# Four maxima in a row, numerators bank by bank, and the first loads on one queue, in an attention and MoE kernel

## The chip, the cores and the metric

The kernel runs on one core of a Trainium2 chip. The metric is the device time of one execution in microseconds. The core has a matrix engine (TensorE, PE in the profile; its weight loads are the row PEld), a vector engine (VectorE, DVE), a scalar engine (ScalarE, ACT), a general one (GpSimd, POOL) and a sequencer that issues transfers (SyncE, SP). Each engine runs its own list of instructions in order, and waits for semaphores of the others. Matmul results lie in PSUM, in banks of 128 x 512 f32 numbers; DVE and ACT read them there.

## The reference

Random-feature attention over 8 batches, 8 heads and 576 tokens, and behind it a mixture of experts in which each token takes one expert:

```python
q_s, k_s = (q * scale, k * scale)
def phi(x):
    h = np.einsum('bhsd,md->bhsm', x, omega) - np.sum(x * x, axis=-1, keepdims=True) / 2.0
    return np.exp(h - np.max(h, axis=-1, keepdims=True)) / np.sqrt(m)
q_p, k_p = (phi(q_s), phi(k_s))
kv = np.einsum('bhsm,bhsd->bhmd', k_p, v)
z = np.sum(k_p, axis=2)
num = np.einsum('bhsm,bhmd->bhsd', q_p, kv)
den = np.einsum('bhsm,bhm->bhs', q_p, z)[..., None] + 1e-06
x = (num / den), heads side by side: 4608 tokens x 512
# MoE: expert_idx = argmax(xn @ en.T / tau); out = gate * (relu(x @ w1[e]) @ w2[e])
```

Per head, omega is 128 x 64: the projection of a token has 128 features. The sum of squares drops out, since the maximum is taken away.

## The kernel before, in words

The 4608 tokens are 36 tiles of 128. Phase 1 is a loop of steps (L623 to L702). Step `i` works on the keys of tile `i` and on the queries of tile `iq = i - 6` (`LAG` is 6), and finishes the numerators of tile `iq - 2`. The eight heads of a tile are two groups of four, `a` = 0 and 1, and each group fills one PSUM bank: 4 x 128 features. So a full step has four banks of projections, here called k0, q1, k1 and q0 (letter and group). The order on each engine is the order of the code, with nothing that reorders it in the loop (`manual_schedule`).

In one full step the engines do this:

- PE: projections of k0 and q1, then of k1 and q0 (`proj`, L322); the products k-features x v of the tile before (`kvmm`, L346); now and then small products (`spare`: the routing counts L456 and L458, the transposed kv L366, its logits L377); transposes of the query features (`qtr`, L392), group 0 into the bank `nu[1]`, group 1 into a bank of the tag "py"; the numerators (`num`, L411), group 0 into `nu[0]`, group 1 into `nu[1]`.
- DVE: `num_out` of the tile before (L424 to L431), the maxima of k0 and q1 (L328), then the list `mid` (reads of the small products: L370, L383, L461, or the reduction over logits L442 to L445), then the maximum of k1, the copy of the transposed queries of group 0 (`qcopy`, L400), the maximum of q0, and the list `ends` (L450 to L452, L464 to L474, L357).
- ACT: four exponentials each (`feats`, L331) for k0 and q1, the `qcopy` of group 1 (L398), then the exponentials of k1 and of q0. An exponential needs the maximum of its bank as its bias.

A bank holds what was put there until its reader is done: the numerators of group 1 need the copy L400, since the transposes of group 0 stand in the same bank `nu[1]`; the next projections need the exponentials of the banks whose places they take. When all keys of half a superblock are in, the accumulated kv is copied to `kvs` (L353, on ACT), and its logits follow over three steps (L357, L366, L370, L377, L383).

`num_out` adds a small constant to the denominators of group 0 and of group 1 (L424, twice), takes one reciprocal over both (L425, 128 x 8), and then multiplies, for each group, the logits (L427) and the 256 numerators (L431).

In the first steps there are no queries yet. Before the loop, SP issues the loads of k (L297), one after the other; ACT issues those of omega (`om`, L572, two halves) and of the first four tiles of v (L306). `om` is scaled on DVE (L575) ahead of the first projection. The MoE follows in phase 2, from about 300 us on.

Of the kernel before, what the change touches and what calls it, by code (L numbers as in the profile page):

```python
# [11 lines left out]
F32 = mybir.dt.float32  # L12
# [4 lines left out]
AF = mybir.ActivationFunctionType  # L17
ALU = mybir.AluOpType
# [4 lines left out]
P = 128  # L23
# [30 lines left out]
def attention_moe(ctx: ExitStack, tc: tile.TileContext, qT, kT, v1, omT, emb, tau, w1q, w2q, xs, out):  # L54
# [225 lines left out]
    with ExitStack() as c1:  # L280
# [11 lines left out]
        def load(i):  # L292

            if i >= NTILE:
                return
            st["k", i] = p1.tile([P, 4, P], F32, name=f"kt{i}", tag="qt" if i in (2, 3) else "kt", bufs=2)
            nc.sync.dma_start(st["k", i], kT[i])  # L297
            sb, u = divmod(i, TPS)
            j = sb * (TPS + 1) + u
            for key, r in [("v", j if u < 4 else j + 1)] + [("v0", j)] * (u == 4):  # L300
                if i in (1, 2):
                    vt = rawp.tile([P, F], F32, name=f"vt{i}", tag="raw_w1")[:, 0 : H * (D + 1)].rearrange("p (h d) -> p h d", h=H)
                else:
                    vt = p1.tile([P, H, D + 1], F32, name=f"vt{i}{key}", tag="vt", bufs=3)

                (nc.scalar if i < 4 else nc.sync).dma_start(vt, v1[r])  # L306
                st[key, i] = vt

        def loadq(i):
# [6 lines left out]
        def proj(*which):  # L316
            for w, i, a, tag in which:
                st["pj" + w, i, a] = ps.tile([P, 4, M], F32, name=f"pj{w}{i}_{a}", tag=tag, bufs=2)
            for c in range(4):
                for w, i, a, _ in which:  # L320
                    r = slice(a * D, (a + 1) * D)
                    nc.tensor.matmul(st["pj" + w, i, a][:, c, :], st[w, i][r, c, :], om[r, :], start=True, stop=True)  # L322

        def feats(which, i, a):

            pj = st["pj" + which, i, a]
            nm = small.tile([P, 4], F32, name=f"nm{which}{i}_{a}", tag=f"nm{which}", bufs=4)
            nc.vector.tensor_reduce(nm, pj, axis=AX.X, op=ALU.max, negate=True)  # L328
            ft = p1.tile([P, 4, M], F32, name=f"ft{which}{i}_{a}", tag=f"ft{which}", bufs=3)
            for h in range(4):  # L330
                nc.scalar.activation(ft[:, h, :], pj[:, h, :], AF.Exp, bias=nm[:, h : h + 1])  # L331
            st["f" + which, i, a] = ft

        def kvmm(i, a, b):
            sb, u = divmod(i, TPS)
            ft = st["fk", i, a]
            vt = st["v0", i] if (u, b) == (4, 0) else st["v", i]
            begin = u == 4 * b
            if begin:
                kva[sb, b, a] = ps.tile([P, 4, D + 1], F32, name=f"kva{sb}_{b}_{a}", tag=f"kv{a}")  # L340
            acc = kva[sb, b, a]
            for h in range(4):


                for c in range(0, P, 64):
                    nc.tensor.matmul(  # L346
                        acc[c : c + 64, h, :], ft[:, h, c : c + 64], vt[:, 2 * h + a, :],
                        start=begin and h == 0, stop=u == 4 + 4 * b and h == 3,
                    )
            if u == 4 + 4 * b:  # L350
                if a == 0:
                    kvs[sb, b] = p1.tile([P, H, D + 1 + E], F32, name=f"kvs{sb}_{b}", tag="kvs", bufs=2)
                nc.scalar.activation(kvs[sb, b][:, 4 * a : 4 * a + 4, 0 : D + 1], acc, AF.Copy)  # L353

        def kv_dense(sb, b):
            kvc = rawp.tile([P, F], F32, name=f"kvc{sb}_{b}", tag="raw_w1")[:, 0:DM].rearrange("p (h d) -> p h d", h=H)
# [59 lines left out]
        def num_out(i):  # L416
            g, gi = divmod(i, G)
            st["xr", i] = xr = p1.tile([P, PAY], F32, name=f"xr{i}", tag="xr", bufs=6)
            nc.gpsimd.tensor_copy(xr[:, PAY - 1 :].bitcast(I32), ids[:, i : i + 1])
            if gi == 0:  # L420
                st["lg", g] = small.tile([P, G, H, E], F32, name=f"lg{g}", tag="lg", bufs=1)
            rr = small.tile([P, 2, 4], F32, name=f"rr{i}", tag="rr", bufs=3)
            for a in range(2):
                nc.vector.tensor_scalar(rr[:, a], pn[a][:, :, D], EPS, None, op0=ALU.add)  # L424
            nc.vector.reciprocal(rr, rr)  # L425
            for a in range(2):
                nc.vector.tensor_tensor(  # L427
                    st["lg", g][:, gi, 4 * a : 4 * a + 4],
                    pn[a][:, :, D + 1 :], rr[:, a].unsqueeze(2).to_broadcast([P, 4, E]), op=ALU.mult,
                )  # L430
                nc.vector.tensor_tensor(  # L431
                    xr[:, 0:DM].rearrange("p (h a d) -> p a h d", a=2, d=D)[:, a],
                    pn[a][:, :, 0:D], rr[:, a].unsqueeze(2).to_broadcast([P, 4, D]), op=ALU.mult,
                )
# [133 lines left out]
        c1.enter_context(tc.manual_schedule(engines={ET.PE, ET.Pool}))  # L568

        om = once.tile([P, M], F32, name="om")  # L570
        for a in range(2):
            nc.scalar.dma_start(om[a * D : (a + 1) * D, :], omT)  # L572
        for i in range(4):
            load(i)
        nc.vector.tensor_scalar(om, om, SCALE, None, op0=ALU.mult)  # L575
# [47 lines left out]
        for i in range(NTILE + LAG + 1):  # L623
            iq = i - LAG
            if i < 2 or i >= 4:
                load(i + (4 if i < 2 else 2))
            loadq(iq + 2)
            if iq - 3 * GPICK - 6 == 3:
                prow = [nc.values_load(
                    firsti[0:1, t : t + 1], engines=[ET.SP], min_val=t * P, max_val=(E - 1) * REG + t * P,  # L630
                    skip_runtime_bounds_check_because=WHY) for t in range(NPRE + 1)]
                for t in range(NPRE):
                    xload(t, prow[t], xgp[t])
            ks, qs = i < NTILE, 0 <= iq < NTILE
            if ks and qs:
                pairs = [("k", i, 0, "py"), ("q", iq, 1, "py")], [("k", i, 1, "px"), ("q", iq, 0, "px")]
            elif ks:
                pairs = [("k", i, a, ("px", "py")[i % 2]) for a in range(2)], []
            else:
                pairs = [("q", iq, a, "px") for a in (1, 0)] if qs else [], []  # L640
            filling = i > NTILE
            proj(*pairs[0])
            proj(*pairs[1])
            if later is not None:
                num_out(later)
            for p in pairs[0][: 1 if i < LAG else 2]:
                feats(*p[:3])
            if 0 <= i - 1 < NTILE:
                sb, u = divmod(i - 1, TPS)
                for b in range(2 if i < LAG and u == 4 else 1):  # L650
                    for a in range(2):
                        kvmm(i - 1, a, b or int(u > 4))
            if i < LAG:
                feats(*pairs[0][1][:3])
            late = bool(spare.get((i,)))
            go(spare, i)
            if later is not None and later % G == G - 1 and later < NTILE - 1:
                steps = routed(later // G)

                for d, key in ((mid, i), (ends, i), (spare, i + 1), (mid, i + 1), (ends, i + 1), (ends, i + 2), (ends, i + 3)):  # L660
                    key = min(key, NTILE + LAG)
                    at(d, key).append((next, steps, None))
            go(mid, i)
            if not qs and iq >= 2:
                num(iq - 2)
            if iq >= 1:

                for a in (1, 0) if late else (0, 1):
                    qtr(iq - 1, a, not ks)
                qcopy(iq - 1, 1, True)  # L670
            if 0 <= i - 1 < NTILE and u == 4 and i >= LAG:
                for a in range(2):
                    kvmm(i - 1, a, 1)
            for p in pairs[1][:1]:
                feats(*p[:3])
            if iq >= 1:
                qcopy(iq - 1, 0, False)
            for p in pairs[1][1:]:
                feats(*p[:3])
            if filling:  # L680
                filled(1 if i <= NTILE + 2 else 2)
            if filling:
                filled(1 if i > NTILE + 2 else 0)
            if 0 <= i - 1 < NTILE:
                if u in (4, 8):
                    b = u // 4 - 1
                    at(ends, i).append((kv_dense, sb, b))
                    at(spare, i + 1).append((kv_turn, sb, b))
                    at(mid, i + 1).append((kv_turned, sb, b))
                    at(spare, i + 2).append((kv_logits, sb, b))  # L690
                    at(mid, i + 2).append((kv_logits_out, sb, b))
            later = iq - 2 if iq >= 2 else None
            if qs and iq >= 2:
                num(iq - 2)
            go(ends, i)
            if filling:
                filled(1)
            n = iq - 3 * GPICK - 6
            if 1 <= n < 2 * NQ + 1:
                at(ends, i + 1).append((first_split, n - 1))  # L700
            if 0 <= n < 2 * NQ:
                first_weights(n)  # L702
# [433 lines left out]
```

## Time and profile before

| | us |
|---|---|
| median of 3 runs (714.92 to 718.11) | 716.06 |
| the profiled execution's own time | 715.37 |
| its span in the profile | 713.7 |
| PE busy in the span | 666.7 (93%) |
| DVE busy | 571.1 (80%) |
| ACT busy | 418.2 (59%) |

The span is the time from the first to the last instruction; 1.67 us of the execution lie around it. Busy shares are averages over stages with different limits: the page's 40 slices show PE at nine tenths or more in most of the span, at six and eight in the first two slices, and at seven and eight in five of the slices around the passage from phase 1 to phase 2. Times below are microseconds from the start of the span.

### The profile page before, as it was taken

Reading aid. Unit: us, or ns where it says so; the run is one execution under the profiler, and the core shown is the slowest. Engines: PE = TensorE matmul, PEld = TensorE weight load, DVE = VectorE, ACT = ScalarE, POOL = GpSimd, SP = SyncE. Lnnn points to the kernel's source line nnn. Section 1 sums busy time; section 2 is a strip of 40 time slices with the busy share of each in tenths; the row PEclk is TensorE's granted clock in tenths of the full one; section 3 lists DMA queues with packets and bytes.
Section 4 is the critical chain, followed back from the end, with each engine's and each line's share of the span. In section 5 each row is a group of like instructions: output and inputs, shape, how many; then the busy total and the mean of one; then the engine's idle time right before and its main releaser. Section 6 shows DMA issues by size and latency. Waiting matters only on the chain. (4 is left out here: it accounts for less than half of the span.)

```text
span 713.7 us, 17997 instructions
## 1 busy us (share of the span) xinstructions
PE 666.7 (93%) x5977; PEld 553.1 (77%) x5978; DVE 571.1 (80%) x1134; ACT 418.2 (59%) x1074; POOL 301.9 (42%) x296
## 2 busy tenths in 40 slices
PE   6899999998998888799999999999999999999994
PEld 5788888887787767588878888788888888878872
DVE  3478888887888756177899999999999998899961
ACT  5687787786887440285456556564746555655530
POOL 2000222221556313265464655546455464554643
PEclk9999999999999999999999999999999999999998
DMA  6434655546772203886978779787887878878730
GB/s 228 131 126 135 195 167 153 193 166 230 242 260 92 75 32 115 299 254 147 231 213 221 209 204 210 214 228 194 224 192 215 219 206 206 217 218 209 181 104 34
DMA packets 142377, 131.86 MB, mean 185 GB/s; under 512 B 106758, under 2 KB 106886, under 8 KB 142288
## 3 DMA queue, kind: packets, MB, share of 16 engines
q1 hardware_dynamic: 135232, 109.17, 56.2%
q0 software_dynamic: 6320, 20.38, 7.6%
q8 instruction: 55, 0.90, 0.5%
q10 hardware_dynamic: 736, 1.13, 0.4%
q14 instruction: 34, 0.28, 0.1%
HBM read 83.78 MB, written 21.97 MB: 148 GB/s over the span
## 5 line engine op out<-in xcount | busy, mean ns | idle before, releaser
L208 POOL TENSOR_TENSOR w1l<-raww,w1h 128x1024 f32 x34 | 89.6, 2637 | 160.9 <-DVE w1h L207 160.6
L885 DVE COPY wd<-t 128x1024 uint16<-128x1024 uint16 x68 | 115.0, 1695 | 1.0 <-DMA t<-pl 1.0
L242 PE MATMUL nu<-w2h,hh 128*128 (+1 forms) x288 | 113.9, 396 | 0.7 <-POOL w2l L208 0.6
L242 PE MATMUL nu<-w2l,hh 128*128 (+1 forms) x288 | 113.6, 395 | 0.0
L242 PE MATMUL nu<-w2h,hl 128*128 (+1 forms) x288 | 113.6, 394 | 0.0
L242 PE MATMUL pa<-w1h,xl 128*128 (+1 forms) x280 | 111.1, 397 | 0.9 <-DVE xl L904 0.8
L242 PE MATMUL pa<-w1h,xh 128*128 (+1 forms) x280 | 110.8, 396 | 0.0
L242 PE MATMUL pa<-w1l,xh 128*128 (+1 forms) x280 | 110.5, 395 | 0.0
L331 ACT ACTIVATE ftk<-pjk,nmk 128x128 f32<-128x128 f32 x288 | 82.6, 392 | 43.6 <-DVE nmk L328 41.2
L901 ACT ACTIVATE hh<-wd 128x1024 fp32r<-128x1024 f32 x34 | 36.1, 1062 | 120.5 <-DVE wd L885 116.3
L331 ACT ACTIVATE ftq<-pjq,nmq 128x128 f32<-128x128 f32 x288 | 83.1, 395 | 16.9 <-DVE nmq L328 16.0
L476 POOL DMA_INDIRECT xs<-xr,posi x36 | 35.9, 997 | 120.8 <-DVE rr L425 40.2
L208 POOL TENSOR_TENSOR w2l<-raww,w2h 128x1024 f32 x34 | 82.7, 2431 | 0.7
L322 PE MATMUL pjk<-om,kt 64*128 64x128 f32 x576 | 75.3, 292 | 7.3 <-DVE om L575 5.9
L322 PE MATMUL pjq<-om,qt 64*128 64x128 f32 x576 | 75.5, 284 | 4.6 <-ACT ftq L331 3.9
L322 PEld LDWEIGHTS pjk<-om,kt 64*128 64x128 f32 x576 | 65.7, 195 | 10.2 <-DVE om L575 5.6
L322 PEld LDWEIGHTS pjq<-om,qt 64*128 64x128 f32 x576 | 63.4, 187 | 8.3 <-ACT ftq L331 5.6
L242 PEld LDWEIGHTS pa<-w1h,xl 128*128 128x128 f32 x280 | 52.7, 188 | 16.6 <-DVE xl L904 4.9
L242 PEld LDWEIGHTS nu<-w2h,hh 128*128 128x128 f32 x288 | 54.3, 188 | 14.0 <-POOL w2l L208 1.4
L242 PEld LDWEIGHTS nu<-w2h,hl 128*128 128x128 f32 x288 | 54.2, 188 | 12.7
L242 PEld LDWEIGHTS nu<-w2l,hh 128*128 128x128 f32 x288 | 54.2, 188 | 12.6
L242 PEld LDWEIGHTS pa<-w1l,xh 128*128 128x128 f32 x280 | 52.7, 188 | 12.1
(303 smaller groups left out, 1301.5 us busy)
## 6 DMA issues: line engine op xcount, KB each, us to landing
raww<-w1q SPq DMA_DIRECT2D x38, 512.0 KB
raww<-w2q SPq DMA_DIRECT2D x38, 512.0 KB
kt<-kT SPq DMA_DIRECT2D x36, 256.0 KB
qt<-qT SPq DMA_DIRECT2D x36, 256.0 KB
xgp<-xs SPq DMA_DIRECT2D x20, 260.5 KB
xg<-xs SPq DMA_DIRECT2D x18, 260.5 KB
rf<-w1q SPq DMA_DIRECT2D x4, 512.0 KB
rf<-w2q SPq DMA_DIRECT2D x4, 512.0 KB
```

The costliest lines, as they stand in the source:

```text
L208: il = nc.gpsimd.tensor_tensor(at(l, dp), raw, at(h, dp).bitcast(F32), op=ALU.subtract)
L242: done.append(nc.tensor.matmul(dst, x[:, c * P : (c + 1) * P], ws.rearrange("p o f -> p (o f)"), start=(begin and i == 0 and k == 0), stop ...
L322: nc.tensor.matmul(st["pj" + w, i, a][:, c, :], st[w, i][r, c, :], om[r, :], start=True, stop=True)
L331: nc.scalar.activation(ft[:, h, :], pj[:, h, :], AF.Exp, bias=nm[:, h : h + 1])
L476: w = nc.gpsimd.indirect_dma_start(out=xs, out_offset=bass.IndirectOffsetOnAxis(ap=posi, axis=0), in_=xr, in_offset=None, bounds_check=ROW ...
L885: nc.vector.tensor_copy(to, src)
L901: nc.scalar.activation(hh, wd[:, 0:F], AF.Relu)
```

## The change

- A new function `maxima` holds the reduction alone, and `feats` calls it only if the maximum isn't there yet. In steps with queries (`i >= LAG`) all four maxima are issued directly behind `num_out`; `mid` and the copy L400 stand behind them.
- `num_out` finishes group 0 (constant, reciprocal of 128 x 4, logits, numerators) before it begins group 1; there are two reciprocals of 128 x 4 for one of 128 x 8.
- `om` is loaded on SP's queue directly behind the first k, and the first four tiles of v go to SP's queue too. ACT issues no loads any more.
- The two copies of the first `kvs` (step 5) go from ACT to DVE.

```diff
@@ load @@
             nc.sync.dma_start(st["k", i], kT[i])
+            if i == 0:
+                for a in range(2):
+                    nc.sync.dma_start(om[a * D : (a + 1) * D, :], omT)
...
-                (nc.scalar if i < 4 else nc.sync).dma_start(vt, v1[r])
+                nc.sync.dma_start(vt, v1[r])
@@ feats @@
+        def maxima(which, i, a):
+            st["nm" + which, i, a] = nm = small.tile([P, 4], F32, name=f"nm{which}{i}_{a}", tag=f"nm{which}", bufs=4)
+            nc.vector.tensor_reduce(nm, st["pj" + which, i, a], axis=AX.X, op=ALU.max, negate=True)
+
         def feats(which, i, a):
-            pj = st["pj" + which, i, a]
-            nm = small.tile([P, 4], F32, name=f"nm{which}{i}_{a}", tag=f"nm{which}", bufs=4)
-            nc.vector.tensor_reduce(nm, pj, axis=AX.X, op=ALU.max, negate=True)
+            if ("nm" + which, i, a) not in st:
+                maxima(which, i, a)
+            pj, nm = st["pj" + which, i, a], st["nm" + which, i, a]
@@ kvmm @@
-                nc.scalar.activation(kvs[sb, b][:, 4 * a : 4 * a + 4, 0 : D + 1], acc, AF.Copy)
+                to = kvs[sb, b][:, 4 * a : 4 * a + 4, 0 : D + 1]
+                if (sb, b) == (0, 0):
+                    nc.vector.tensor_copy(to, acc)
+                else:
+                    nc.scalar.activation(to, acc, AF.Copy)
@@ num_out @@
             for a in range(2):
                 nc.vector.tensor_scalar(rr[:, a], pn[a][:, :, D], EPS, None, op0=ALU.add)
-            nc.vector.reciprocal(rr, rr)
-            for a in range(2):
+                nc.vector.reciprocal(rr[:, a], rr[:, a])
                 nc.vector.tensor_tensor(
...
@@ before the loop @@
         om = once.tile([P, M], F32, name="om")
-        for a in range(2):
-            nc.scalar.dma_start(om[a * D : (a + 1) * D, :], omT)
@@ the loop @@
             if later is not None:
                 num_out(later)
+            if i >= LAG:
+                for p in pairs[0] + pairs[1]:
+                    maxima(*p[:3])
             for p in pairs[0][: 1 if i < LAG else 2]:
                 feats(*p[:3])
```

The order on PE and POOL is the same in both kernels. Where the change moves instructions, three places show it.

DVE in step 20 of the loop, ahead of the copy `qp` (L400), before. `nmk` and `nmq` are the maxima of k and q, `kvs` reads the small product L377 from the bank `nu[1]`, `raw` and `mx` are the reduction over logits:

```order
L328 TENSOR_REDUCE nmk_0_2147<-pjk_0_2117 128x4
L328 TENSOR_REDUCE nmq_1_2154<-pjq_1_2118 128x4
L383 COPY kvs_1_1916<-nu_71 128x4x2x8
L442 TENSOR_REDUCE raw_2186<-lg_1885 128x24
L444 TENSOR_REDUCE mx_2188<-raw_2186 128x3
L445 TENSOR_TENSOR raw_2186<-raw_2186,mx_2188 128x24
L328 TENSOR_REDUCE nmk_1_2205<-pjk_1_2127 128x4
L400 COPY qp_0_2212<-nu_71 128x512
L328 TENSOR_REDUCE nmq_0_2214<-pjq_0_2128 128x4
```

The same step on DVE in the changed kernel (its lines are up to 10 higher):

```order
L328 TENSOR_REDUCE nmk_0_2159<-pjk_0_2128 128x4
L328 TENSOR_REDUCE nmq_1_2161<-pjq_1_2129 128x4
L328 TENSOR_REDUCE nmk_1_2163<-pjk_1_2138 128x4
L328 TENSOR_REDUCE nmq_0_2165<-pjq_0_2139 128x4
L393 COPY kvs_1_1930<-nu_71 128x4x2x8
L451 TENSOR_REDUCE raw_2202<-lg_1894 128x24
L453 TENSOR_REDUCE mx_2204<-raw_2202 128x3
L454 TENSOR_TENSOR raw_2202<-raw_2202,mx_2204 128x24
L410 COPY qp_0_2226<-nu_71 128x512
```

The maxima of k1 and q0 have moved ahead of the read of the small product; the copy `qp` has one maximum fewer ahead of it once the small product is there, and one more in all.

DVE in `num_out` at the end of the same step, before (`rr` holds the denominators, `lg` the logits, `xr` the tokens' rows; `nu_70` and `nu_71` are the banks of group 0 and 1):

```order
L424 TENSOR_SCALAR rr_2274<-nu_70 128x4
L424 TENSOR_SCALAR rr_2274<-nu_71 128x4
L425 RECIPROCAL rr_2274<-rr_2274 128x8
L427 TENSOR_TENSOR lg_2273<-nu_70,rr_2274 128x32
L431 TENSOR_TENSOR xr_2271<-nu_70,rr_2274 128x4x64
L427 TENSOR_TENSOR lg_2273<-nu_71,rr_2274 128x32
L431 TENSOR_TENSOR xr_2271<-nu_71,rr_2274 128x4x64
```

The same place in the changed kernel:

```order
L434 TENSOR_SCALAR rr_2286<-nu_70 128x4
L435 RECIPROCAL rr_2286<-rr_2286 128x4
L436 TENSOR_TENSOR lg_2285<-nu_70,rr_2286 128x32
L440 TENSOR_TENSOR xr_2283<-nu_70,rr_2286 128x4x64
L434 TENSOR_SCALAR rr_2286<-nu_71 128x4
L435 RECIPROCAL rr_2286<-rr_2286 128x4
L436 TENSOR_TENSOR lg_2285<-nu_71,rr_2286 128x32
L440 TENSOR_TENSOR xr_2283<-nu_71,rr_2286 128x4x64
```

Seven instructions have become eight, and the first four need the bank of group 0 alone.

SP's first loads before the loop, before (those of `om` and of four tiles of v stand on ACT):

```order
L297 DMA kt_134<-kT 128x512
L297 DMA kt_138<-kT 128x512
L297 DMA kt_142<-kT 128x512
L297 DMA kt_146<-kT 128x512
L579 DMA taub<-tau 8x1
L581 DMA emb_sb<-emb 8x512
```

The same in the changed kernel:

```order
L297 DMA kt_132<-kT 128x512
L300 DMA om<-omT 64x128 x2
L308 DMA vt0v<-v 128x520
L297 DMA kt_138<-kT 128x512
L308 DMA vt_140<-v 128x520
L297 DMA kt_142<-kT 128x512
L308 DMA vt_144<-v 128x520
L297 DMA kt_146<-kT 128x512
L308 DMA vt3v<-v 128x520
```

Three issues now stand between the first k and the second, and four of v have joined the queue.

## Rows read from the trace of the kernel before

**Rows 1.** Busy time by engine of two stretches (PE, PEld, DVE, ACT, POOL), and PE's clock:

```profile
44.99:227.96 182.97, 170.74 (x3149) 152.09 (x3150) 153.97 (x486) 142.07 (x487) 53.27 (x106) 1.00 0.55 181
300.00:713.70 413.70, 401.68 (x1740) 322.66 (x1738) 355.95 (x430) 223.28 (x417) 220.31 (x108) 0.99 0.76 199
```

**Rows 2.** Waits, 44.99 to 227.96: who waited for whom, us in total, times, longest:

```profile
DVE kvs L383 <- PE nu L377: 6.2, 6, 1.2
DVE qp L400 <- PE nu L392: 5.6, 14, 1.1
DVE rr L424 <- PE nu L411: 4.2, 8, 1.2
DVE base L461 <- PE nu L458: 4.0, 5, 1.1
...
PE nu L411 <- DVE qp L400: 3.6, 7, 0.7
PE tr L392 <- ACT ftk L331: 3.4, 6, 1.6
DVE kvts L370 <- PE nu L366: 2.7, 3, 1.8
PE pjq L322 <- ACT ftq L331: 2.5, 7, 0.7
```

**Rows 3.** Timeline, 0 to 8 us: start, duration, engine, line, idle before:

```profile
0.98 1.94 SPq L297 DMA_DIRECT2D kt<-kT  x4
0.98 1.20 ACTq L572 DMA_DIRECT2D om<-omT  x2
...
4.32 0.35 SPq L579 DMA_DIRECT2D taub<-tau  x1
...
5.65 0.23 DVE L575 TENSOR_SCALAR om<-om 128x128 f32<-128x128 f32 x1 [4.46 <-DMA om<-omT]
```

**Rows 4.** Timeline of PE in step 5:

```profile
23.49 1.15 PE L346 MATMUL kva<-vt4v,ftk 128*64 128x65 f32 x32 [1.10 <-ACT kvs L353]
...
25.47 0.37 PE L322 MATMUL pjq<-om,qt 64*128 64x128 f32 x1 [0.41 <-ACT ftk L331]
```

**Rows 5.** Timeline of DVE in step 6:

```profile
29.23 0.69 DVE L370 COPY kvts<-nu 128x512 f32<-128x512 f32 x1 [1.48 <-PE nu L366]
```

**Rows 6.** Timeline of ACT in step 6:

```profile
30.63 1.14 ACT L331 ACTIVATE ftk<-pjk,nmk 128x128 f32<-128x128 f32 x4 [1.21 <-PE pjq L322]
```

**Rows 7.** Timeline of DVE in step 20 (116.00 to 123.19):

```profile
118.43 0.22 DVE L383 COPY kvs<-nu 128x64 f32<-128x64 f32 x1 [1.15 <-PE nu L377]
...
119.42 0.68 DVE L328 TENSOR_REDUCE nmk<-pjk 128x4 f32<-128x512 f32 x1
120.02 0.68 DVE L400 COPY qp<-nu 128x512 f32<-128x512 f32 x1
...
121.80 0.22 DVE L424 TENSOR_SCALAR rr<-nu 128x4 f32<-128x4 f32 x2
122.05 0.20 DVE L425 RECIPROCAL rr<-rr 128x8 f32<-128x8 f32 x1
122.29 0.19 DVE L427 TENSOR_TENSOR lg<-nu,rr 128x32 f32<-128x32 f32 x1
...
122.73 0.18 DVE L427 TENSOR_TENSOR lg<-nu,rr 128x32 f32<-128x32 f32 x1
...
123.19 0.68 DVE L328 TENSOR_REDUCE nmk<-pjk 128x4 f32<-128x512 f32 x1
```

**Rows 8.** Timeline of PE in step 20:

```profile
119.33 0.73 PE L411 MATMUL nu<-kvs,qp 128*64 128x73 f32 x16
120.75 0.73 PE L411 MATMUL nu<-kvs,qp 128*64 128x73 f32 x16 [0.69 <-DVE qp L400]
```

**Rows 9.** Timeline of DVE at 56.78, a denominator whose group came late:

```profile
56.78 0.16 DVE L424 TENSOR_SCALAR rr<-nu 128x4 f32<-128x4 f32 x1 [0.17 <-PE nu L411]
56.98 0.20 DVE L425 RECIPROCAL rr<-rr 128x8 f32<-128x8 f32 x1
```

## The prediction

> **What bounds the kernel now.** I read the busy table by stretch first. In phase 2, from 300 us on, PE is busy for 401.68 of 413.70 us at a granted clock of 0.99 of full speed (2.4 GHz): the stretch is matmul work, and the change puts nothing there. So a microsecond gained in phase 1 should shift phase 2 forward by as much. In the loop's full steps, 44.99 to 227.96, there are 28 steps (9 to 36) of 6.53 us on average. Of these PE is busy for 170.74 / 28 = 6.10, DVE for 153.97 / 28 = 5.50, ACT for 142.07 / 28 = 5.07 [rows 1]. No engine is full, PE is nearest, and the three hold each other up: that is a stage bound by waits.
>
> The table of waits says by whom [rows 2]. DVE stands still for 22.7 us in its five largest waits, all of them for PE: 6.2, 4.0 and 2.7 for small products (`kvs`, `base`, `kvts`), 5.6 for the transposes that it copies, 4.2 for numerators. PE in turn stands still for 3.6 us because the copy `qp` isn't there when the numerators of group 1 want it, for 3.4 because a transpose needs a bank that the exponentials of k still read, and for 2.5 because a projection needs a bank of the exponentials of q. The timeline of step 20 shows how the first two meet. DVE stops for 1.15 us until the small product L377 is there, although two maxima with data ready stand behind it; `qp` then starts at 120.02, behind one of these, and PE, done with group 0's numerators, waits 0.69 us until 120.75 [rows 7, 8].
>
> **The change part by part.**
>
> *Four maxima first.* A maximum takes 0.60 of DVE from start to next start (119.42 to 120.02). In step 20 those of k1 and q0 would fill 1.15 us of waiting almost to the end; the read of `kvs` stays at 118.43, the reduction runs until 119.42, and `qp` starts there, not at 120.02 [rows 7]. PE's numerators of group 1 would then start at about 120.15 for 120.75 [rows 8]. Seven waits of this kind sum to 3.6 us, the longest 0.7 [rows 2]; each can shrink by up to 0.60, and I leave 0.1 of each: 3.6 - 0.7 = 2.9 gained. The floor is the copy itself, which the numerators must follow. In plain steps without a small product `qp` gets a maximum more ahead of it, but there DVE waited for the transposes (14 waits, 5.6 us, 0.4 each) [rows 2]: the maximum fills that, and the 0.2 that stick out lie beside group 0's numerators on PE, which take 0.73 [rows 8].
>
> The 3.4 us of PE for exponentials of k hang on when the maximum of k0 is there, that is on when `num_out` ends. In the seven steps above DVE ends its step up to 0.9 earlier (0.6 from the filled wait, and the maximum of q0 that stood behind `qp` is done too, less what `num_out` gains in length, below). I count 2.0 of the 3.4, bounds 0 and 3.4. The 2.5 us for exponentials of q I leave: there ACT's own row of work decides, sixteen exponentials and a copy in a step. Sum for the 28 steps: -4.9. Bounds: 0 if DVE's gain is eaten, and 3.6 + 3.4 = 7.0 gained if both waits go whole.
>
> *Numerators bank by bank.* Before, from the first instruction of `num_out` to the next maximum is 121.80 to 123.19, 1.39 us: 0.25 for two denominators, 0.24 for the reciprocal with its result's way, 0.44 and 0.46 for the two groups [rows 7]. After, each group has a denominator (0.20 from start to the reciprocal's start, [rows 9]), a reciprocal of four columns and 0.45. The trace has no 128 x 4 reciprocal: it lies between 0.16, what another four-column instruction takes [rows 9], and 0.20 for eight [rows 7], and I take 0.17 and 0.04 of way, 0.21. So 0.86 per group, 1.70 in all with rounding: +0.31 of DVE in a step (+0.23 to +0.37). Against it, group 0's half can run while PE still works at group 1. Where DVE waits for the numerators (8 waits, 4.2 us, [rows 2]) only the second half, 0.86, stands behind the end of the wait instead of 0.20 + 0.24 + 0.44 + 0.46 = 1.34: 0.48 sooner. Where it doesn't wait, the 0.31 lie in slack: a step then has 5.50 + 0.31 = 5.81 of DVE in 6.53 - 0.18 = 6.35 us. I take 0 for this part, with -0.48 x 8 = -3.8 and +0.31 x 28 = +8.7 as the ends.
>
> The Trainium skill speaks against this part: its page "VectorE: DVE Perf Modes", section "Rules for kernel authors", says to minimise the count of DVE instructions, since each pays its pipeline's flush whatever it waits for. The trace bears it out, in that an eight-column reciprocal still holds DVE for 0.24 [rows 7]; what it would give as a result of its own is the slower rival below.
>
> *The start.* `om` is issued at 0.98 on ACT and is there at about 5.6, when DVE can scale it at 5.65; the first projection follows. The first k, issued at the same moment on SP, has landed by 4.32, when SP gets past the wait for it [rows 3]. With `om` next to it on SP, issued one and two issues later (1.94 / 4 = 0.49 each, [rows 3]), 64 KB behind 256 KB, I expect it at 4.6: -1.0. Bounds: +1.5 (`om` no sooner than now would be 0; the second k, below) and -1.3 (together with k). The second k has three more issues ahead of it on SP. I cost that at nothing, since it is wanted only behind the first tile's projections; if that cover is gone, the price is 3 x 0.49 = 1.5.
>
> In the page "DMA: Bandwidth & Descriptors", section "Issuing engines are not separate DMA queues", the Trainium skill says that transfers started by different engines run on the same 16 DMA engines and that spreading them saves only time on the sequencers. By it the order would matter and the queue would not; the trace's 1.3 us between k and `om`, issued together, isn't told by it either way.
>
> *First kv copies on DVE.* In step 5 PE waits 1.10 us for ACT's copy of `kva`, and 0.41 at 25.47 for exponentials that stand behind the copies [rows 4]. A 128 x 260 copy lies between 0.22 (64 columns) and 0.68 (512) [rows 7], about 0.45; the two also delay the maximum of k1 on DVE. -0.7, bounds 0 and -1.1.
>
> *First full steps.* In step 6 the maximum of k1 stood behind `kvts`, which waited 1.48 until 29.23 [rows 5]; ACT stood still 1.21 us until 30.63 for it [rows 6]. With the maximum in the wait, ACT goes straight on: -1.2. Step 8 has the same form with `kvs`, worth 0.4 (0 to 0.6). Sum -1.6, bounds 0 and -1.8.
>
> *Sum.* -1.0 - 0.7 - 1.6 - 4.9 = -8.2 on the profiled execution's 715.37: 707.2. The median of the runs stands 0.69 above that execution, so 707.9.
>
> **Rivals.**
>
> *DVE becomes the bound (slower).* Place: `num_out` at the end of each step, between PE's numerators and the maximum of k0 on which ACT, and through its banks PE, depend. Price: 0.31 x 28 = 8.7, less 1.0 + 0.7 + 1.6 = 3.3 of the start: +5.4, 721.5. It decides from the point where the maxima fill less than 0.31 of the 22.7 / 28 = 0.81 us that DVE waits per step. For it: PE and DVE are within 0.6 of each other [rows 1]. Against it: in step 20 the fill alone is over 1 us [rows 7].
>
> *Nothing in the steady steps.* What the maxima give, the longer `num_out` takes back; only the start's 3.3 is left: 712.8. For it: the waits for small products are 6 + 5 + 3 = 14 [rows 2], so that about 14 of the 28 steps have none to fill, and pay 0.31. Against it: there DVE waits for numerators or transposes anyway [rows 2].
>
> *More than counted.* All 7.0 of PE's two waits go: 707.9 - 2.1 = 705.8, and with the 2.5 of the third, because DVE runs ahead from step to step, 703.3.
>
> *The start brings nothing.* `om` arrives no earlier behind k on the same queue: 708.9. For it: it is in line behind 256 KB; against it: it landed after k in any case [rows 3]. Chance 0.25, in any of the cases above.
>
> **How the numbers follow.** The forecast, 707.9, has 0.57, with a range of its own from 705 to 711; more than counted 0.14; nothing in the steady steps 0.21; slower 0.08. Within 0.5% (3.6 us) is what a measurement of this kernel can't tell from no change. So faster is the first two and a small part of the third, which lies at the bound: 0.75; same 0.17; slower 0.08. The range of 8 in 10 leaves out the slower case and the best tail: 703.5 to 714.
>
> **What would show it.** Right: the waits of DVE for `kvs`, `base` and `kvts` (12.9 us together) fall to under 4; PE's wait for `qp` from 3.6 to under 1; the first matmul stands at about 4.9 instead of 5.9; the wait of 1.10 in step 5 goes; the first step of phase 2 comes 7 to 9 us earlier and phase 2 is as long as before. Wrong: the step of the loop stays at 6.5 while DVE's busy time rises by 8 us, or the gain of phase 1 comes back as waits between 228 and 300 us, where I count nothing, or phase 2 gets longer.

## The result, and the profile after

| | before | changed |
|---|---|---|
| median of 4 runs, us | 716.89 (714.92 to 718.11) | 709.35 (707.70 to 709.72) |
| profiled execution's own time, us | 715.37 | 709.05 |
| span, us | 713.7 | 707.5 |

The ratio is 0.9898, with a 95% interval of 0.9881 to 0.9915. On the 716.06 from which the forecast was made that is 7.3 us less, where 8.2 were forecast; the two medians of the table lie 7.5 apart. Timed beside the kernel before two more times, the changed kernel gave 0.9887 (0.9866 to 0.9909) and 0.9897 (0.9874 to 0.9919).

The first look is again at busy time by stretch. The stretches answer to those of [rows 1]: the full steps 9 to 36 with a little of the end, and phase 2 (columns as there):

```profile
41.69:220.90 179.21, 168.29 (x3153) 147.84 (x3153) 158.80 (x514) 138.88 (x488) 53.94 (x107) 1.00 0.56 185
...
293.00:707.50 414.50, 402.00 (x1740) 323.04 (x1740) 354.81 (x430) 224.97 (x419) 220.25 (x108) 0.99 0.75 200
```

PE has as much work in phase 2 as it had (402.00 for 401.68), and the gain was made ahead of it: phase 2's first product of `w1l` and `xh` starts at 301.00 before and at 294.95 after, 6.05 sooner, and from there to the end it is 412.70 us before and 412.55 after. (The windows from 300.00 and from 293.00 don't begin at the same instruction.) In the steps DVE is busy for 158.80 us, 4.8 more than before, in 3.8 us less of time.

The start of the changed kernel, the timeline (start, duration, engine, line, idle before):

```profile
4.50 0.23 DVE L582 TENSOR_SCALAR om<-om 128x128 f32<-128x128 f32 x1 [3.31 <-DMA om<-omT]
4.78 3.57 PE L324 MATMUL pjk<-om,kt 64*128 64x128 f32 x30 [4.78 <-DVE om L582]
...
```

`om` is there 1.15 us sooner than at 5.65 [rows 3], and the first matmul starts at 4.78. DVE in steps 5 and 6 shows what became of [rows 4, 5]:

```profile
20.81 0.90 DVE L361 COPY kvs<-kva 128x260 f32<-128x260 f32 x2
21.62 0.68 DVE L328 TENSOR_REDUCE nmk<-pjk 128x4 f32<-128x512 f32 x1
...
27.37 0.69 DVE L380 COPY kvts<-nu 128x512 f32<-128x512 f32 x1 [0.21 <-PE nu L376]
```

and PE in step 5:

```profile
20.08 2.37 PE L352 MATMUL kva<-vt4v,ftk 128*64 128x65 f32 x64
...
23.61 0.37 PE L324 MATMUL pjq<-om,qt 64*128 64x128 f32 x1 [0.75 <-ACT ftk L337]
```

The two copies take 0.81 from the first's start to the next instruction, 0.40 each, and PE runs its 64 products of that step without the gap of 1.10. It then waits 0.75 for exponentials, where it waited 0.41 [rows 4]. The read `kvts` waits 0.21, where it waited 1.48.

Now the waits of the steady steps, 41.69 to 220.90, against [rows 2] (us in total, times, longest):

```profile
DVE qp L410 <- PE nu L402: 6.7, 10, 0.8
...
PE tr L402 <- ACT ftk L337: 2.5, 6, 1.4
DVE nmk L328 <- PE pjq L324: 2.3, 6, 0.5
PE nu L421 <- DVE posi L483: 2.0, 3, 0.7
DVE rr L434 <- PE nu L421: 2.0, 6, 0.5
...
PE pjq L324 <- ACT ftq L337: 1.8, 6, 0.4
PE nu L402 <- DVE run L471: 1.8, 8, 0.3
...
DVE kvts L380 <- PE nu L376: 0.6, 1, 0.6
```

DVE's waits for `kvs` and `base`, 6.2 and 4.0 before, are gone from the list, and `kvts` fell from 2.7 to 0.6: of 12.9 us of standing for small products 0.6 are left. DVE's five waits sum to 9.3, down from 22.7; one of 2.3 has come, where the first maximum of a step waits for its projection. PE's wait of 3.6 for the copy `qp` is now the line with `posi`, 2.0: the copy is in flight there, and the view names an instruction behind it on DVE. PE has a new wait too, 1.8 for `run`: the read of the routing counts now stands behind four maxima, and PE wants to put transposes into the same bank. Step 20 answers to [rows 7, 8], first DVE and then PE:

```profile
112.27 0.68 DVE L328 TENSOR_REDUCE nmk<-pjk 128x4 f32<-128x512 f32 x1
...
113.47 0.21 DVE L393 COPY kvs<-nu 128x64 f32<-128x64 f32 x1
...
114.44 0.69 DVE L410 COPY qp<-nu 128x512 f32<-128x512 f32 x1
...
117.46 0.69 DVE L328 TENSOR_REDUCE nmk<-pjk 128x4 f32<-128x512 f32 x1
```

```profile
114.33 1.59 PE L421 MATMUL nu<-kvs,qp 128*64 128x73 f32 x32
```

The step begins at 111.07. `kvs` follows the four maxima without a wait, the copy `qp` starts 3.37 us into the step instead of 4.02, and PE runs both groups of numerators in one row of 32 without the 0.69. The step takes 6.39 us, where it took 7.19.

Of the three waits of PE that are left for `qp`, two are new. In steps 17 and 26 there is no small product to wait for, the reduction over logits stands in `mid`, and `qp` now comes behind one maximum more. PE's numerators in step 17, before and after:

```profile
100.08 1.25 PE L411 MATMUL nu<-kvs,qp 128*64 128x73 f32 x32
```

```profile
94.67 0.73 PE L421 MATMUL nu<-kvs,qp 128*64 128x73 f32 x16
96.08 0.73 PE L421 MATMUL nu<-kvs,qp 128*64 128x73 f32 x16 [0.68 <-DVE posi L483]
```

Each of these two steps became some 0.4 longer (6.25 for 5.83 in step 17).

The largest part of the gain is not in the list of waits. It leaves out a standstill of one bank's matmuls while those of another keep PE busy. Here are PE's projections alone, L322 or the line that answers to it, from the first maximum of step 9 to that of step 35 (busy time of PE, then of PEld): the kernel before, the changed kernel, and two kernels of the experiments below, the one that moves the maxima alone and the one that changes the start alone:

```profile
44.99:215.30 170.31, 61.98 (x844) 55.77 (x845) 1.00 0.57 187
```

```profile
41.69:208.23 166.54, 56.84 (x843) 51.00 (x844) 1.00 0.58 192
```

```profile
43.05:207.41 164.36, 56.85 (x838) 51.12 (x840) 1.00 0.59 194
```

```profile
44.79:213.77 168.98, 61.82 (x844) 55.49 (x845) 1.00 0.58 189
```

The same projections take some 5 us less wherever the maxima are moved. In step 20 it looks like this, before (ACT, then PE) and after:

```profile
120.20 1.14 ACT L331 ACTIVATE ftk<-pjk,nmk 128x128 f32<-128x128 f32 x4 [0.59 <-DVE nmk L328]
121.39 1.14 ACT L331 ACTIVATE ftq<-pjq,nmq 128x128 f32<-128x128 f32 x4
122.42 0.38 PE L322 MATMUL pjk<-om,kt 64*128 64x128 f32 x2
122.58 0.37 PE L322 MATMUL pjq<-om,qt 64*128 64x128 f32 x1
```

```profile
115.34 1.24 ACT L337 ACTIVATE ftq<-pjq,nmq 128x128 f32<-128x128 f32 x4
116.73 0.38 PE L324 MATMUL pjq<-om,qt 64*128 64x128 f32 x2
116.84 0.27 PE L324 MATMUL pjk<-om,kt 64*128 64x128 f32 x1
```

PE issues projections of k and of q by turns. Before, ACT waited 0.59 for the maximum of k1, so the exponentials of q0 ended at 122.53; the second projection of q, which needs their bank, began at 122.58, when those of k had gone ahead alone since 122.42. After, the exponentials end at 116.58, ahead of the second pair, and the two go by turns throughout. From the first projection of the step to the products behind them it was 2.25 us (121.42 to 123.67), and is 1.99 (115.84 to 117.83).

To see where the gain arose, I set the start of the first maximum of a step in both kernels side by side, with two later profiled executions: the changed kernel again, and the changed kernel with one reciprocal:

| step | before | changed | changed, third time | one reciprocal |
|---|---|---|---|---|
| 0 | 8.04 | 6.89 (-1.15) | 6.71 (-1.33) | 6.62 (-1.42) |
| 5 | 21.23 | 20.07 (-1.16) | 20.28 (-0.95) | |
| 6 | 26.46 | 24.67 (-1.79) | 24.88 (-1.58) | 24.39 (-2.07) |
| 9 | 44.99 | 41.69 (-3.30) | 41.90 (-3.09) | 41.57 (-3.42) |
| 35 | 215.30 | 208.23 (-7.07) | 205.74 (-9.56) | 205.89 (-9.41) |

### The profile page after: what moved, and what is told of

Same layout as the page of the kernel before. It is cut to its first block, busy times and chain, and to the rows that moved or that the text cites. A ratio compares the mean times of both kernels' runs of the same rounds, so it can differ in the third digit from the quotient of the medians.

```text
span 707.5 us, 18035 instructions
## 1 busy us (share of the span) xinstructions
PE 662.0 (94%) x5977; PEld 547.3 (77%) x5978; DVE 576.5 (81%) x1172; ACT 414.8 (59%) x1072; POOL 302.0 (43%) x296
## 5 line engine op out<-in xcount | busy, mean ns | idle before, releaser
L324 PE MATMUL pjk<-om,kt 64*128 64x128 f32 x576 | 73.7, 290 | 4.9 <-DVE om L582 4.8
L324 PE MATMUL pjq<-om,qt 64*128 64x128 f32 x576 | 71.2, 282 | 3.9 <-ACT ftq L337 3.1
```

## The experiments

Twelve runs were made, in three groups of four; each group shared one chip, and each ratio is to the kernel before on that chip. Whatever differs from chip to chip may be in a comparison of two groups; the changed kernel itself gave 0.9887 to 0.9898 in the three times it was timed. Each profile is one execution.

**Each part alone.** First the maxima:

```diff
# on the kernel before
+            if i >= LAG:
+                for p in pairs[0] + pairs[1]:
+                    maxima(*p[:3])
```

> The kernel before with the four maxima moved ahead, and nothing else. Theory A (the parts add up, the longer num_out lies in slack): the steps 6 to 8 give 1.6 us and the steady steps 3 to 5, so about 5.5 us less than before (ratio 0.992). Theory B (the maxima carry the steady gain alone and the split of num_out costs in steps without a wait): 6.5 us less or more (0.991 or below), and the start of step 18 against step 15 loses nothing against before, where the changed kernel loses 0.86 us.

Measured: 0.988 (0.9848 to 0.9912). From step 9 to step 35 it takes 164.36 us, where the kernel before takes 170.31: 5.95 less. The ratio is the one that Theory B gives, and the maxima alone carry the whole gain of the steady steps. But from step 15 to 18 this kernel loses 0.63 us against the kernel before, though it has no split: the 0.86 that the changed kernel loses there is mostly not the split's, and this detail of Theory B fell. Then the split of `num_out`:

```diff
# on the kernel before
-            nc.vector.reciprocal(rr, rr)
-            for a in range(2):
+                nc.vector.reciprocal(rr[:, a], rr[:, a])
```

> The kernel before with num_out bank by bank, and nothing else. Theory A: within 1 us of before (ratio 0.9985 to 1.0015). Theory B: DVE's chain per step is 0.31 longer where it does not wait for numerators, so 1.5 to 4 us more than before (1.002 to 1.006).

Measured: 1.0071 (1.0048 to 1.0094), 5.1 us slower, where Theory B said 1.5 to 4; the lower end of the interval is within it. Its waits of DVE, steps 9 to 34:

```profile
DVE kvs L383 <- PE nu L377: 5.2, 6, 1.1
...
DVE base L460 <- PE nu L457: 4.1, 8, 0.7
...
DVE rr L424 <- PE nu L411: 0.2, 1, 0.2
```

Without the maxima moved, the waits for small products stay, and the wait for numerators, 4.2 before [rows 2], is 0.2: the longer `num_out` has eaten it. From step 9 to step 35 this kernel takes 172.17 us, 1.86 more than before, and that is within Theory B. Its profile shows 715.64 us, the fastest of its twelve executions (median 718.66), and doesn't show where the others lose more. Last the start:

```diff
# on the kernel before: om and v on SP's queue, and
+                if (sb, b) == (0, 0):
+                    nc.vector.tensor_copy(to, acc)
```

> The kernel before with omega and v on SP's queue and the first kv copies on DVE. Both theories: 1.15 us from omega and 0.6 from the copies, 1.8 us less than before (ratio 0.9975), the step of the loop unchanged. The rival that the gain of the start is lost in later waits: 1.000.

Measured: 0.9961 (0.9935 to 0.9987); the interval holds the expected 0.9975 and is clear of 1.000. In its profile the gain of 1.70 at step 7 is 0.19 at step 8, and the loss is PE's clock (windows, columns as in [rows 1]; the clock is the third number from the end):

```profile
28.90:31.16 2.26, 0.87 (x8) 0.49 (x5) 1.72 (x3) 2.22 (x9) 0.00 (x0) 0.98 0.55 195
31.16:34.75 3.59, 3.59 (x47) 3.37 (x49) 0.00 (x0) 2.01 (x8) 0.00 (x0) 0.54 0.18 63
```

PE had stood still for most of 2.26 us, waiting for exponentials; then the granted clock was 0.54 for 3.59 us, near the lower level of 1.2 GHz. The kernel before shows 1.00 in that step. From step 9 to step 35 this execution then takes 168.98 us, 1.33 less than before, although it leaves the code of these steps alone. So it doesn't show by what way the start's gain reaches the end; and a difference of 1.3 us between the loops of two profiles is not beyond what the same code gives.

**The split, with the maxima moved.** The changed kernel with one reciprocal again:

```diff
# on the changed kernel
-                nc.vector.reciprocal(rr[:, a], rr[:, a])
+            nc.vector.reciprocal(rr, rr)
+            for a in range(2):
```

> The changed kernel with one reciprocal of 128 x 8 behind both denominators again, as before. Theory A: equal to the changed kernel within 0.7 us. Theory B: 1.5 to 3 us faster than the changed kernel (ratio to before 0.986 to 0.988 where the changed kernel has 0.990). Theory C (bank by bank is what shortens the wait between numerators and maxima in every step): 2 us or more slower than the changed kernel (0.993).

Measured: 0.986 (0.9827 to 0.9892), which looked like Theory B. But the changed kernel hadn't been timed beside it, so it ran again in the second group:

> The changed kernel itself, beside the three others of this call on one chip. Theory B (the split of num_out costs some 2 us of loop time): ratio to before 0.989 to 0.991.

Measured: 0.9887 (0.9866 to 0.9909), and its loop was 2.7 us shorter from step 9 to 35 than in the first profile (163.88 for 166.54). That took the ground from Theory B, and in the third group both ran on one chip:

> The changed kernel itself, beside the next three on one chip: ratio to before 0.988 to 0.991.

> The changed kernel with one reciprocal for both groups, on the same chip as the changed kernel this time. Theory B (the split costs 2 us or more): 0.984 to 0.987, clear of the changed kernel's. Theory A (it lies in slack, and what the two runs on different chips showed was a difference of chips): within 0.2% of the changed kernel.

Measured: 0.9897 (0.9874 to 0.9919) for the changed kernel and 0.9876 (0.9851 to 0.99) with one reciprocal, medians of 705.75 and 704.99 us. That is 0.2% with intervals that overlap: Theory A, the split is worth nothing that can be measured here. A cost of 1 to 2 us isn't excluded, since both ratios with one reciprocal lie below all three of the changed kernel. The profiles don't decide it either: from step 9 to step 35 the one reciprocal takes 164.32 us, between the 163.84 and the 166.54 of the changed kernel. The waits of DVE in the two, first with one reciprocal, then the changed kernel, say why:

```profile
DVE rr L434 <- PE nu L421: 8.9, 26, 0.7
```

```profile
DVE rr L434 <- PE nu L421: 1.3, 5, 0.4
```

With the maxima moved and one reciprocal, DVE comes early and waits for numerators 26 times in the stretch. The split uses 7.6 us of this wait to do group 0's half and pays with 0.31 more work per step: the one makes good the other.

**The length of `num_out`.** Shorter, by leaving the constant out of the denominators, and longer, by two needless products:

```diff
# shorter
-                nc.vector.tensor_scalar(rr[:, a], pn[a][:, :, D], EPS, None, op0=ALU.add)
-            nc.vector.reciprocal(rr, rr)
+                nc.vector.reciprocal(rr[:, a], pn[a][:, :, D])
# longer
             nc.vector.reciprocal(rr, rr)
+            for _ in range(2):
+                nc.vector.tensor_scalar(rr, rr, 1.0, None, op0=ALU.mult)
```

> The changed kernel with num_out in the order of before, and the constant of the denominators left out: two reciprocals of 128 x 4 read the denominators directly, so that num_out is some 0.25 us shorter than with one reciprocal for both. Theory B (the length of num_out itself is priced at about a quarter of what it adds to VectorE): 1 to 2 us faster than the changed kernel with one reciprocal, which had 0.986: 0.983 to 0.985. Theory C (not the length but the order of the two groups costs): 0.986.

> The changed kernel with one reciprocal for both groups, and two needless multiplications by 1 of 128 x 8 behind it: num_out 0.4 to 0.5 us longer, 11 to 14 us of VectorE in the 28 steps. Theory B: 3 to 6 us slower than the changed kernel with one reciprocal (0.986), so 0.990 to 0.995. Theory C: within 1 us of 0.986. If VectorE is the bound already: the whole 11 to 14 us, 1.002 or more.

Measured: 0.9815 (0.9791 to 0.9838), a little better than Theory B, and 1.0193 (1.0159 to 1.0227). DVE of the shorter one, from the second reciprocal to the next maximum:

```profile
114.25 0.18 DVE L434 RECIPROCAL rr<-nu 128x4 f32<-128x4 f32 x1 [0.16 <-PE nu L421]
...
115.40 0.69 DVE L328 TENSOR_REDUCE nmk<-pjk 128x4 f32<-128x512 f32 x1
```

and of the longer one:

```profile
127.54 0.41 DVE L437 TENSOR_SCALAR rr<-rr 128x8 f32<-128x8 f32 x2
127.98 0.19 DVE L439 TENSOR_TENSOR lg<-nu,rr 128x32 f32<-128x32 f32 x1
```

The two products hold DVE for 0.44. From step 9 to step 30 the longer kernel takes 142.03 us, the one with one reciprocal, on another chip, 132.74: 9.29 in 21 steps, 0.44 a step, the whole price. The shorter kernel takes 130.07, 0.13 a step less, with 1.15 us behind group 1's numerators instead of 1.34. (The changed kernel itself takes 131.90 on their chip; against it the longer one has 0.48 a step more, the shorter one 0.09 less.) So the way from the numerators of group 1 to the next maximum is on the path of the loop: what is added there is paid in full, and what is taken off pays in part. That is the third expectation, the whole price. The longer kernel lost another 11 us from step 30 to 35, where its granted clock is 0.92 on average, so its ratio is above what the price alone gives.

**The new wait for the counts.** The two reads of the counts ahead of the fourth maximum, in the steps that have them:

```diff
# with one reciprocal
-                for p in pairs[0] + pairs[1]:
+                for p in (pairs[0] + pairs[1])[: 3 if base else 4]:
...
             go(mid, i)
+            if i >= LAG and base:
+                for p in pairs[1][1:]:
+                    maxima(*p[:3])
```

> The changed kernel with one reciprocal for both groups, and in the 11 steps with routing counts the two reads of the counts ahead of the maximum of q0 (behind three maxima, not four). In the changed kernel TensorE's transposes of group 0 wait for the read of the counts for 1.8 us in 8 steps. If that wait is on the path: 1 to 2 us faster than 0.986, so 0.983 to 0.985. If it lies beside other waits: 0.986.

Measured: 0.9898 (0.9873 to 0.9924), beside 0.9887 for the changed kernel on that chip. The wait of PE for `run` is gone from its profile and nothing came of it (from step 9 to step 35 163.69 us, where the changed kernel has 163.88 on that chip): it lay beside other waits. One reciprocal without this change didn't run on that chip.

**Both banks at once.** `num_out` in four instructions, with the two banks as one tile, and then the reduction over logits moved as well:

```diff
# with one reciprocal
-    nu = [ps.tile([P, 512], F32, name=f"nu{a}") for a in range(2)]
+    nu2 = ps.tile([P, 2, 512], F32, name="nu")
+    nu = [nu2[:, a] for a in range(2)]
...
+            nc.vector.tensor_scalar(rr, both[:, :, :, D], EPS, None, op0=ALU.add)
+            nc.vector.reciprocal(rr, rr)
+            nc.vector.tensor_tensor(..., both[:, :, :, D + 1 :], ...)
+            nc.vector.tensor_tensor(..., both[:, :, :, 0:D], ...)
# and then
-                for d, key in ((mid, i), (ends, i), (spare, i + 1), ...
+                for d, key in ((ends, i), (ends, i), (spare, i + 1), ...
```

> The changed kernel with num_out in four instructions that each read both banks of numerators at once (constant 128 x 8, reciprocal 128 x 8, logits 128 x 64, numerators 128 x 512). VectorE's part is 1.15 to 1.25 us by the durations of 0.20, 0.24, about 0.15 and about 0.6, where the changed kernel has 1.69. If the length of num_out is what counts, as the kernel without the constant suggests: 3 to 6 us faster than the changed kernel, 0.981 to 0.985. If it counts more that group 0's half can run while TensorE still works at group 1: slower than the changed kernel.

> The same, and the reduction over the logits (three instructions, 1.0 us, in every third step) behind the copy of the transposed queries, not ahead of it. In the changed kernel TensorE's numerators of group 1 stand 0.56 longer than they must in about eight such steps. If that is on the path: 2 to 4 us faster than with both banks alone. If VectorE's whole work is the bound: the same as that.

Measured: 1.0188 (1.0165 to 1.0211) and 1.0235 (1.0208 to 1.0263), far on the wrong side of what was hoped for. Slower had been expected for the case that it counts most to do group 0's half early, and DVE does wait more for numerators (22.5 us for `rr` below); but another cause stands ahead of that. DVE's part came out as worked out (1.18 us from the constant to the next maximum). What went wrong shows on PE in step 20 of the first, and behind it in the waits:

```profile
119.77 1.25 PE L422 MATMUL nu<-kvs,qp 128*64 128x73 f32 x32 [0.79 <-DVE posi L484]
```

```profile
DVE rr L435 <- PE nu L422: 22.5, 23, 2.3
...
PE nu L422 <- DVE qp L411: 8.2, 11, 0.8
PE nu L422 <- DVE posi L484: 7.9, 11, 1.1
```

All 32 numerators wait for the copy `qp`, not the 16 of group 1 alone: the first matmul of group 0 carries the wait for DVE, where with two tiles the first of group 1 does. The dependence goes by tile here, the copy reads the half that group 0 doesn't write, and PE loses the 0.6 us of group 0 that used to cover the copy: 16.1 us of waits. How much of the 12 us that its loop is longer (176.17 for 163.84) comes from this and how much from DVE's wait isn't shown apart. These two kernels say nothing on the length of `num_out`, nor does the second on the place of the reduction: it wasn't tried on two tiles.

## Why the prediction was right

**The start and the first steps** came out term by term. `om` and the first projection: -1.15 in the first profile and -1.0 to -1.4 in the others, for -1.0; the two kernels that leave the start as it was show -0.3 there, so that much is variation. The copies on DVE: from -1.16 at step 5 to -1.79 at step 6, -0.63 for -0.7, with 0.40 for one copy where 0.45 was taken; of the 1.10 gained, 0.34 went into the longer wait for exponentials. Steps 6 to 8: -1.51 for -1.6, and -1.65 with the maxima alone. The second k didn't hold PE up: the lead is still 1.10 at step 1 and 1.17 at step 2. The Trainium skill, page "DMA: Bandwidth & Descriptors", section "Issuing engines are not separate DMA queues", lets one expect only sequencer time from the choice of engine; here the same two transfers landed 1.15 us sooner with SP as the issuer behind k, and what of that is the queue and what the order, no run shows.

**The four maxima** gave the forecast sum, but only in part by its terms. The steady steps gave -3.8 in the first profile and -6.4 and -6.5 in the two others, for -4.9; alone the maxima gave -5.95. DVE's waits filled as forecast. PE's wait for `qp` was to give 2.9 and gave 1.6 (3.6 to 2.0): six of its seven waits left the list, that of step 35 stayed, and in two steps the fourth maximum ahead of `qp` made a new one. The wait for the exponentials of k was to give 2.0 and gave 0.9 (3.4 to 2.5), and the wait for `run`, which the sum doesn't have, took 1.8 back. What made up for it is the term that I put at nothing, the exponentials of q, because ACT's own row of work was to decide there. ACT wasn't at work throughout: in step 20 it stood 0.59 for the maximum of k1, and with the maxima moved PE's projections shrank by 5.1 us. That the sum came out near is luck to this extent, and the rival of more than counted had the right reason for a part of it.

**The split of `num_out`** was priced right, 1.69 us measured from 40.00 to 41.69 for 1.70, and its 0 in sum agrees with what was measured. The reason was half of the truth. I set 8 waiting steps of the profile before against 28 that pay. With the maxima moved DVE would wait in 26, and that is the cover. Alone, on a DVE that comes late, the same edit costs 0.7%: the rival with DVE as the bound had the sign right for the split without the maxima, though 5.1 us is short of its 8.7. The rule of the Trainium skill on the count of instructions (page "VectorE: DVE Perf Modes", section "Rules for kernel authors") agrees with 1.0071 there, and with the maxima moved no run shows it.

**The tail** was costed at nothing, and in the first profile it gave 0.9 back: -7.07 at step 35, -6.2 at the end. So phase 2 begins 6.05 sooner, not the 7 to 9 that were named as a sign of being right. Two windows each show it, a stretch in which PE mostly waits and what it does next: first of the kernel before, then of the changed kernel, then of the changed kernel in its third profile.

```profile
231.65:235.15 3.50, 1.17 (x17) 0.97 (x16) 2.81 (x11) 1.94 (x6) 1.21 (x2) 1.00 0.30 89
235.15:240.19 5.04, 5.04 (x60) 4.18 (x60) 3.65 (x14) 2.67 (x9) 1.70 (x10) 0.66 0.11 43
```

```profile
224.59:228.37 3.78, 1.17 (x18) 0.98 (x17) 3.04 (x12) 1.93 (x6) 1.21 (x2) 0.91 0.35 108
228.37:234.63 6.26, 6.26 (x59) 5.36 (x60) 4.28 (x17) 2.77 (x9) 2.01 (x11) 0.51 0.05 19
```

```profile
222.08:225.86 3.78, 1.17 (x18) 0.97 (x17) 3.04 (x12) 1.94 (x6) 1.21 (x2) 1.00 0.34 108
225.86:229.33 3.47, 3.47 (x59) 2.96 (x59) 3.30 (x13) 2.66 (x9) 0.69 (x5) 1.00 0.09 35
```

In all three PE is busy for 1.17 us of the first window. Behind it the same 59 or 60 matmuls take 5.04 us at a granted clock of 0.66, 6.26 at 0.51, and 3.47 at 1.00, in the last two by one and the same program. In the first profile the lead over the kernel before is 6.78 us ahead of these matmuls and 5.56 behind them. POOL's scatter of the rows of late tiles, for which SP waits before it goes on to the loads of phase 2, starts 5.57 sooner (264.01 for 269.58), and phase 2 6.05. So the loss in the tail of the first profile fits the clock after a standstill, which falls in one execution and not in the next; the link from there to phase 2 is read from these times, and no run shows it alone.

What stays open is why the loop of the changed kernel took 166.5 us in the first profile and 163.9 in two others, at a granted clock of 1.00 throughout. The ratio to the kernel before agrees within 0.11% in all three timings, so it doesn't touch the result.

## What to carry to other kernels

A wait in the profile is worth filling with work that is ready and would follow anyway: 12.9 us of waits by DVE, filled with maxima, gave 4 to 6 us of loop. A list of waits doesn't hold all that an engine loses: where its busy time falls for the same instructions, a wait went that the list didn't show. What an added instruction costs depends on whether its engine comes early or late at that place, so an edit that is harmful alone can be free beside another; count the waits that the other edit will leave, not those of the profile before. And kernels that are to be compared at a few tenths of a per cent belong side by side: the same kernel with one reciprocal gave 0.986 in one group and 0.9876 in another.

## What was not expected of the hardware

- The granted clock of TensorE fell to about half around a standstill of PE of 2.61 us in one execution of the changed kernel and stayed at 1.00 in another, and the next 59 matmuls took 6.26 us instead of 3.47. In the kernel with the start alone it fell behind 2.26 us of which PE was busy for 0.87.
- One instruction on DVE that reads two PSUM banks side by side works at the usual pace: 128 x 512 in 0.68 us, as a copy of 128 x 512 from one bank, and 128 x 64 in 0.22. A reciprocal of 128 x 4 takes 0.18 from SBUF or PSUM, where 128 x 8 takes 0.20.
